# Moving pads, a mask and a sign guard between ScalarE, VectorE and GpSimd in a top-32 attention pipeline, with a new order of its steps

## The chip, the cores and the metric

The kernel runs on one core of a Trainium2 chip, as one launch. The metric is the device time of that launch in microseconds. TensorE is called PE here, its weight loads PEld, VectorE DVE, ScalarE ACT, GpSimd POOL and SyncE, which issues the transfers, SP, as the profile does. L305 is line 305 of the kernel before.

## What is computed

Three stages follow each other: attention that keeps the 32 largest scores of each row, a soft mixture of experts, and a two-layer network with a piecewise quadratic activation.

```python
B, H, S, D = 4, 8, 576, 64                     # attention
scores = (q @ k.T) / 8
kth = 32nd largest of each row
scores = where(scores >= kth, scores, -1e9)
x = softmax(scores) @ v                        # to (2304, 512)

logits = x @ phi                               # 8 experts x 4 slots
d = softmax(logits, axis=0); slots = d.T @ x
slots = relu(slots @ w1[e]) @ w2[e]            # 512 -> 1024 -> 512
x = softmax(logits, axis=1) @ slots

h = x @ w_in                                   # 512 -> 2048
g = where(h >= 1, h, where(h <= -1, 0, (h + 1)**2 / 4))
out = g @ w_out                                # 2048 -> 512
```

The weights `w_in` and `w_out` reach the chip as 64-bit numbers, so a step of the kernel turns them into 32-bit ones.

## The kernel before

**Tiling.** A unit of attention is a pair of heads, 16 in all (`NPAIR`), and a row group of 128 queries: groups 0 to 3 hold 128 queries of each of the two heads (j = 0, 1), group 4 the last 64 of both. The work on a group is cut into steps, each with a letter, a group and mostly a head: S11 is the scores of group 1 (there the second digit is a half of the columns), P30 the penalty of group 3, head 0.

**The steps of a group.** S: scores on PE (`op_s`). C: copy to SBUF on ACT (`op_c`, L296). G: the eight largest of each of seven segments on DVE (L305). L: from these, the 24 largest, on DVE (L312, L310). [...] X: scores once more on PE, with the masked ones pushed far down (`op_x`). Y: the next eight on DVE (L418), of which the last is the 32nd largest. Groups 3 and 4 (`BY_V`) take another way to Y: POOL multiplies scores and mask (V, L406). K: eight extra columns, the pad, from the count, so that ties and short counts come out right (`op_k`): on ACT for the V path and POOL's masks (L428), else on DVE (L430).

**The second half.** N: the largest score times -0.125, on POOL (L353), for the exponential. B: the 32nd largest times 2^100, on POOL (L441). P: a penalty for all that is smaller, on ACT (L445). U: its subtraction, on POOL (L448). E: exponential on ACT (L451). T, Q, R: transposes on PE and their copies on ACT. A: product with v on PE. H: copy of the result on ACT (L513). lD and lN, once per pair: the sum of each row plus 1e-9 and its reciprocal, on DVE (L532, L533), then the division on POOL (L536). The steps "m" are the softmax over the tokens of a batch, after its fourth pair; the last batch is treated apart.

**The conversion.** c0 to c6, once per pair, turn a 128 x 512 piece of `w_in` to 32 bits (`narrow`): Abs, low word and Sign on ACT (L225, L227, L229), a guard of the size and the reassembly on POOL (L231, L235, L237), a shift on DVE (L233). Its input is loaded by SP (L203), and its result stored (L217).

**What sets the order.** PE, ACT, DVE and POOL carry out their instructions in the order in which the steps are called, and that is the list `ORDER`, written out in the code. One pass through the list is a frame; the letter behind a step says how many frames it lags. So a frame mixes steps of up to five pairs:

```python
for frame in range(first, NPAIR + last + 1):
    for name, k in order:
        if frame == first == k and name[0] == "c":
            held.append(name)
        elif 0 <= frame - k < NPAIR:
            emit(name, frame - k)
            if name == "C20":
                while held:
                    emit(held.pop(0), 0)
    for name in held:
        emit(name, 0)
```

In the first frame the conversion's steps are held until C20 has been called or the frame ends. After the frames come the last batch's softmax (`moe_last`), the experts, the mixing and the network. Their weights are loaded by SP in one list (`wload`), each as soon as a buffer is given back; most buffers come free at the end of attention.

Of the kernel before, what the change touches and what calls it, by code (L numbers as in the profile page):

```python
# [64 lines left out]
Q40d B1c U01c M30c S40c E00c T41d C40c X20c G40c M31c P10c R4d S00b K21c P11c X21c me U10c Q41d  # L65
C00b Y20c E01c V30c T00c K30c Q00c S01b c4b C01b G00b c2b E10c Y21c U11c A40d T01c R0c B2c c5b
L4c V31c A41d S10b Q01c C10b Y30c P20c H4d X00b K31c E11c U20c S11b C11b T10c G01b A00c Q10c lDd
lNd c6b P21c A01c N3c E20c T11c Y31c H0c R1c M40c Q11c B3c U21c S20b V40c L0b K40c G10b C20b
M00b lYd lXd lEd P30c T20c S21b lCd z4b E21c A10c Q20c C21b A11c G11b T21c M01b K00b P31c H1c
N4c U30c Y40c L1b N1b O01b S30b G20b md R2c B4c me K01b X01b Q21c E30c A20c T30c md me M10b U31c  # L70
c0a C30b md me Y00b G21b A21c S31b Y01b E31c X10b L2b Q30c M11b P40c O11b H2c K10b c3a K11b me
T31c C31b B0b N0b U40c md M20b M21b P00b
# [6 lines left out]
def kernel_body(tc, qT, kT, vP, phi, w1, w2, w_in, w_out, out, fast, flag):  # L79
# [128 lines left out]
    def conv_op(i, k):  # L208
# [4 lines left out]
        if k == 2 and i + 1 < NCV:  # L213
            conv_load(i + 1)
# [4 lines left out]
    def narrow(x64, tr, sg, ops):  # L219
# [138 lines left out]
    def op_m(u, j):  # L358
# [4 lines left out]
        t = st[u]["t0"] + j  # L363
# [68 lines left out]
    def kth(u):  # L432
        return st[u]["l8"][:, :, PADS - 1] if fast else st[u]["top"][:, :, TOPK - 1]

    def op_b(u):
        n, t = width[u[1]], st[u]["t0"]
        if u[1] in BY_V:
            st[u]["kb"] = kth_all[:, t:t + n]
        else:
            st[u]["kb"] = p_small.tile([P, 2], F32, name="kb", tag="kb")  # L440
        nc.gpsimd.tensor_scalar(st[u]["kb"][:, :n], kth(u)[:, :n], BIG, None, op0=ALU.mult)  # L441

    def op_p(u, j):
# [6 lines left out]
    def op_e(u, j):  # L450
        nc.scalar.activation(row(u, j), row(u, j), AF.Exp, bias=st[u]["nm"][:, j:j + 1], scale=0.125)  # L451
# [282 lines left out]
    calls = dict(S=op_s, C=op_c, G=op_g, L=op_l, N=op_n, M=op_m, O=op_o, X=op_x, Y=op_y, K=op_k, B=op_b, P=op_p, U=op_u,  # L734
# [93 lines left out]
    if fast:  # L828
        cmp = p_moe.tile([P, NTILE], F32, name="cmp")
# [451 lines left out]
```

## Time and profile before

| | |
|---|---|
| timed runs | 803.58, 805.63, 807.99 us (median 805.63) |
| the profiled execution | 807.38 us, span 805.5 us, mean granted clock 0.983 of full |
| busy, share of the span | PE 94%, PEld 68%, DVE 81%, ACT 80%, POOL 57% |
| until 490 us (attention) | PE, DVE, ACT and POOL mostly at 0.9 or more, in tenths of a slice |
| 524 to 585 us | the 16 DMA engines full, 402 GB/s |
| from 585 us | PE 213 of 220 us |

The shares of the whole span are a mean over these stretches. A window gives the busy time of each engine in one stretch, overlaps counted once; what is left of the stretch is idle time, and the list of waits says which instruction of which engine ended most of it. Short gaps between small instructions are not listed there. Mean durations of a group of instructions overlap with those of their neighbours on the same engine by up to a tenth of a microsecond. PE's ends are modelled, so its busy time is an upper limit.

### The profile page before, as it was taken

The page shows a single profiled execution, that of the slowest core. Times are in us where ns is not written, and L with a number is a line of the kernel's source. Part 1 is how long each engine was busy: PE and PEld are TensorE (multiplying, and loading weights), DVE is VectorE, ACT ScalarE, POOL GpSimd, SP SyncE. Part 2 cuts the span into 40 slices and gives each one's busy share as a digit, 9 for nine tenths or more (in the row PEclk, how much of TensorE's full clock was granted, in tenths as well). Part 3 has the DMA queues.
Part 4 walks back from the last instruction along what each step waited for, and adds up shares of the span by engine and source line. Part 5 has one row for each costly group of instructions (what it writes and reads, how often), then busy time and mean ns, then how long its engine had stood idle before and what let it go on. Part 6 is the DMA issues. An engine that isn't in the chain of part 4 may idle for free.

```text
span 805.5 us, 15892 instructions
## 1 busy us (share of the span) xinstructions
PE 758.6 (94%) x5006; PEld 549.9 (68%) x5022; DVE 649.2 (81%) x2937; ACT 644.2 (80%) x1392; POOL 456.9 (57%) x482
## 2 busy tenths in 40 slices
PE   3799999999999999999999998898899999999996
PEld 1367677686777677767677777432477788888885
DVE  3999999999999999999999995153478876666662
ACT  3699999999999999999999997244399974545542
POOL 2699999998999999899999894002022200000000
PEclk9799999999999999999999999699999999999999
DMA  7234124224213222202202126599910020101001
GB/s 233 73 106 145 59 87 143 68 82 143 85 60 144 80 70 92 79 14 92 78 18 92 43 87 192 163 386 405 409 71 1 0 81 1 39 1 40 33 8 43
DMA packets 31726, 81.51 MB, mean 101 GB/s; under 512 B 5648, under 2 KB 6544, under 8 KB 31632
## 3 DMA queue, kind: packets, MB, share of 16 engines
q1 hardware_dynamic: 31344, 79.94, 28.2%
q8 instruction: 41, 0.67, 0.3%
q14 instruction: 53, 0.43, 0.2%
q10 hardware_dynamic: 288, 0.46, 0.2%
HBM read 71.25 MB, written 8.91 MB: 100 GB/s over the span
## 4 chain that ended last, share of the span: by engine, by line
PE 57%; DVE 18%; ACT 16%; POOL 4%; DMA 3%; issue 2%; SPq 1%; ACTq 0%; POOLq 0%; DVEq 0%
PE o_ps L1091 24%; PE av_ps L500 6%; PE s_ps L281 5%; PE pt_ps L459 5%; DVE cand L305 4%; ACT pen L445 4%; DVE l L418 4%; PE x_ps L281 3%; ACT ssb L296 3%; DVE cand L310 3%; DVE top L312 2%; PE h_ps L1055 2%; PE h L924 2%; POOL ssb L448 2%; DVE den L532 2%; DMA w<-in_moe_w_dram 2%
## 5 line engine op out<-in xcount | busy, mean ns | idle before, releaser
L1091 PE MATMUL o_ps<-whl,ghl 128*128 128x512 f32 x864 | 215.9, 394 | 0.0
L448 POOL TENSOR_TENSOR ssb<-ssb,pen 128x576 f32<-128x576 f32 x141 | 182.9, 1297 | 13.8 <-ACT pen L445 9.6
L1091 PEld LDWEIGHTS o_ps<-whl,ghl 128*128 128x128 f32 x864 | 160.7, 188 | 34.5 <-DVE ghl L1075 0.3
L305 DVE MAX8 cand<-ssb 128x8 f32<-128x82 f32 (+1 forms) x1008 | 165.1, 228 | 1.9 <-ACT ssb L296 1.9
L500 PE MATMUL av_ps<-v_sb,ptb 128*128 128x65 f32 (+1 forms) x1280 | 144.1, 262 | 0.0
L500 PEld LDWEIGHTS av_ps<-v_sb,ptb 128*128 128x128 f32 (+1 forms) x1280 | 138.8, 182 | 0.3
L281 PE MATMUL s_ps<-kt,qt 64*128 64x288 f32 x512 | 98.5, 462 | 15.5 <-ACT ssb L296 11.2
L451 ACT ACTIVATE ssb<-ssb,nm 128x576 f32<-128x576 f32 x141 | 111.8, 793 | 1.3 <-POOL ssb L448 0.9
L1057 ACT ACTIVATE rg<-h_ps,half 128x384 f32<-128x384 f32 x96 | 55.7, 580 | 67.8 <-PE h_ps L1055 67.8
L459 PE MATMUL pt_ps<-ident,ssb 128*128 128x128 f32 x640 | 100.9, 280 | 2.3 <-ACT ptb L475 0.9
L296 ACT COPY ssb<-s_ps 128x576 f32<-128x576 f32 x144 | 94.3, 655 | 7.4 <-PE s_ps L281 6.2
L1042 POOL TENSOR_TENSOR tr_l<-tr_l 128x512 int32<-128x512 int32 x16 | 20.9, 1307 | 130.1 <-PE so L947 46.2
L1063 DVE SCALAR_TENSOR_TENSOR rg<-h_ps,rg 128x384 f32<-128x384 f32 x96 | 53.3, 556 | 48.3 <-ACT rg L1058 48.3
L459 PEld LDWEIGHTS pt_ps<-ident,ssb 128*128 128x128 f32 x640 | 71.9, 146 | 29.8 <-ACT ptb L478 7.1
L369 POOL TENSOR_SCALAR mb<-ssb,top 128x576 bf16<-128x576 f32 x48 | 83.2, 1733 | 3.6 <-DVE top L312 3.6
L475 ACT COPY ptb<-pt_ps 128x512 f32<-128x512 f32 x128 | 77.6, 606 | 1.2 <-PE pt_ps L459 1.2
L418 DVE MAX8 l<-x_ps 128x8 f32<-128x584 f32 x96 | 73.0, 762 | 6.0 <-PE x_ps L400 6.0
L445 ACT ACTIVATE pen<-ssb,kb 128x576 bf16<-128x576 f32 x96 | 75.6, 788 | 2.1 <-POOL kb L441 1.8
L281 PEld LDWEIGHTS s_ps<-kt,qt 64*128 64x128 f32 x512 | 41.2, 191 | 51.2 <-ACT ssb L296 27.7
L312 DVE MAX8 top<-cand 128x8 f32<-128x56 f32 x432 | 73.2, 206 | 0.1
L406 POOL TENSOR_TENSOR w<-ssb,mb 128x576 f32<-128x576 f32 x48 | 61.5, 1282 | 0.1
L1075 DVE TENSOR_TENSOR ghl<-rg,ghl 128x384 fp32r<-128x384 f32 x96 | 55.2, 575 | 6.3 <-PE h_ps L1055 0.5
(220 smaller groups left out, 1306.8 us busy)
## 6 DMA issues: line engine op xcount, KB each, us to landing
w<-in_moe_w_dram SPq DMA_DIRECT2D x52, 512.0 KB, 6.4
x<-in_moe_w_in_dram SPq DMA_DIRECT2D x16, 512.0 KB, 4.9
w<-in_moe_w_out_dram SPq DMA_DIRECT2D x16, 512.0 KB, 10.2
w<-in_moe_w_dram SPq DMA_DIRECT2D x24, 256.0 KB, 4.7
kt<-in_k_dram SPq DMA_DIRECT2D x15, 360.0 KB, 3.0
v_sb<-in_v_dram SPq DMA_DIRECT2D x16, 325.0 KB, 4.8
qt<-in_q_dram SPq DMA_DIRECT2D x15, 320.0 KB, 3.5
out_dram<-o_sb SPq DMA_DIRECT2D x17, 256.0 KB, 2.5
```

The costliest lines, as they stand in the source:

```text
L281: nc.tensor.matmul(o, q[us], k[us, c:c + o.shape[-1]], start=True, stop=True, tile_position=(j * D, 0), skip_group_check=True)
L296: nc.scalar.copy(ssb[:, 0] if u[1] == NR else ssb[:, :, hf], st.pop((u, hf))[:, :, :HS])
L305: nc.vector.max(st[u]["cand"][:, j, 8 * g:8 * g + 8], row(u, j)[:, S * g // NSEG:S * (g + 1) // NSEG])
L312: nc.vector.max(t8, cand)
L369: nc.gpsimd.tensor_scalar(kept(u, j), row(u, j), t_u, None, op0=ALU.is_ge)
L418: nc.vector.max(st[u]["l8"][:, j], src)
L445: nc.scalar.activation(pen, row(u, j), AF.Relu, bias=st[u]["kb"][:, j:j + 1], scale=-BIG)
L448: nc.gpsimd.tensor_tensor(row(u, j), row(u, j), st.pop((u, "pen", j)), op=ALU.subtract)
L451: nc.scalar.activation(row(u, j), row(u, j), AF.Exp, bias=st[u]["nm"][:, j:j + 1], scale=0.125)
L459: nc.tensor.transpose(pt[:, c, :], pr[:, c0:c0 + P], ident)
L500: nc.tensor.matmul(o, pj[:, c, sl], v_sb[:, 4 * jj + c, :], start=False, stop=(c == NR - 1), skip_group_check=True)
L1091: nc.tensor.matmul(pos[t][n], a[:, sl], w, start=(f == 0 and k == 0), stop=(f == NF - 1 and k == 2))
```

## The change

Pads that ACT made are made on POOL (K for POOL's masks and for the V path), as a product with the count and a sum, in one instruction. The scaled maximum N goes; B multiplies the largest and the 32nd largest by -0.125 and 2^100 in one product with a table `factor`, into a tile `kn`. For that, Y writes its eight beside the 24 in `top`. One more mask, group 2, head 0, is made on POOL, so ACT counts it (O20). In the conversion, Abs and the guard on POOL go; DVE adds and subtracts 768 so that values under the guard become 0, ACT takes the sign of that, and the shift reads its input directly. The sum for den gets an accumulator that nothing reads. The counts are kept in smaller tables. The list is new.

```diff
-MASK_POOL = ((0, 1), (1, 1), (2, 1))
+MASK_POOL = ((0, 1), (1, 1), (2, 0), (2, 1))
+TINY = 1.5 * 2.0 ** 9
+NTOP = 6
 ORDER = '''
-X11c R3d me G30c Q31d E40d Y10c A30d G31c U00c c1b A31d P01c O21c Y11c L3c K20c H3d me N2c T40d
+A20c T30c C30b U31c O11b U40c Q30c Y01b A21c E31c L2b H2c S31b X10b B0b K10b C31b T31c c0a md
...
+    factor = p_moe.tile([P, 2, 2], F32, name="factor")
+    nc.vector.memset(factor[:, :, 0], -0.125)
+    nc.vector.memset(factor[:, :, 1], BIG)
...
-        if k == 2 and i + 1 < NCV:
+        if k == 4 and i + 1 < NCV:
             conv_load(i + 1)
...
             if k == 0:
-                nc.scalar.activation(tf, hf, AF.Abs)
+                nc.vector.tensor_scalar(sg, hf, TINY, TINY, op0=ALU.add, op1=ALU.subtract)
...
             elif k == 2:
-                nc.scalar.activation(sg, hf, AF.Sign)
-            elif k == 3:
-                nc.gpsimd.tensor_scalar(tf, tf, 2.0 ** -15, None, op0=ALU.max)
+                nc.scalar.activation(sg, sg, AF.Sign)
             elif k == 4:
-                nc.vector.tensor_scalar(t, t, 3, None, op0=ALU.logical_shift_left)
+                nc.vector.tensor_scalar(t, x64[:, :, 1], 3, None, op0=ALU.logical_shift_left)
...
-    def op_n(u):
-        n = width[u[1]]
-        nm = st[u]["nm"] = p_small.tile([P, 2], F32, name="nm", tag="nm")
-        nc.gpsimd.tensor_scalar(nm[:, :n], st[u]["top"][:, :n, 0], -0.125, None, op0=ALU.mult)
...
-        nc.vector.max(st[u]["l8"][:, j], src)
+        nc.vector.max(st[u]["top"][:, j, TOPU:], src)
...
         if v or (u[1], j) in MASK_POOL:
-            nc.scalar.activation(pad, ranks[:, 1 + v], AF.Identity, bias=ends_of[:, v:v + 1], scale=n)
+            nc.gpsimd.tensor_scalar(pad, ranks[:, 1 + v], n, (1.0, BIG)[v], op0=ALU.mult, op1=ALU.add)
         else:
-            nc.vector.tensor_scalar(pad, ranks[:, 0], n, 0.0, op0=ALU.subtract, op1=ALU.add, accum_out=ends_of[:, 2:3])
+            nc.vector.tensor_scalar(pad, ranks[:, 0], n, 0.0, op0=ALU.subtract, op1=ALU.add, accum_out=unread)
...
-        nc.gpsimd.tensor_scalar(st[u]["kb"][:, :n], kth(u)[:, :n], BIG, None, op0=ALU.mult)
+        nc.gpsimd.tensor_tensor(st[u]["kn"][:, :n], st[u]["top"][:, :n, 0:TOPK:TOPK - 1], factor[:, :n], op=ALU.mult)
...
-            nc.vector.tensor_scalar_add(den, xu_of[pi][:, :, D], 1e-9)
+            nc.vector.tensor_scalar(den, xu_of[pi][:, :, D], 1e-9, 0.0, op0=ALU.add, op1=ALU.add, accum_out=unread)
...
             if k == "P":
+                if j == 0:
+                    nm = st[u]["nm"] = p_small.tile([P, 2], F32, name="nm", tag="nm", bufs=2)
+                    n = width[r]
+                    nc.gpsimd.tensor_scalar(nm[:, :n], st[u]["top"][:, :n, 0], -0.125, None, op0=ALU.mult)
```

The new list has 168 entries for 173. Three places of it matter here. The first is ACT at the start of the program. Before:

```order
L578 COPY same<-pick_78 128x32 x4
L225 ACTIVATE tr<-x_191 128x512
L227 ACTIVATE tr<-x_191,two 128x512
L296 COPY ssb<-s_ps 128x2x288 x2
L229 ACTIVATE sg<-x_191 128x512
L296 COPY ssb<-s_ps 128x2x288 x4
```

After (L303 is the copy of scores, L232 the low word, L234 the Sign):

```order
L574 COPY same<-pick_78 128x32 x4
L303 COPY ssb<-s_ps 128x2x288 x5
L232 ACTIVATE tr<-x_192,two 128x512
L234 ACTIVATE sg<-sg 128x512
L381 ACTIVATE ones,cnt_all<-mb 128x576
```

The Abs and the low word of the first conversion stood ahead of the first copy of scores; the Abs is gone, and the low word and the Sign now stand behind the fifth copy. On DVE, at the same place, the rounding (L230) and the shift (L236) of the first conversion now follow the scans of the first group (L312), ahead of its selection (L319):

```order
L312 MAX cand<-ssb 128x8 x14
L230 TENSOR_SCALAR sg<-x_192 128x512
L236 TENSOR_SCALAR tr<-x_192 128x512
L319 MAX top<-cand 128x8 x2
L317 MATCH_REPLACE cand<-top,cand 128x56 x2
```

Before, the only one of the two, the shift, stood ahead of all scans. The third place is POOL in the middle of a frame, in the new order (L371 is a mask, L427 a pad, L444 the subtraction U, L437 the product B):

```order
L371 TENSOR_SCALAR mb<-ssb,top 128x576
L444 TENSOR_TENSOR ssb<-ssb,pen 128x576 x2
L437 TENSOR_TENSOR kn<-top,factor 128x4
L427 TENSOR_SCALAR mb<-ranks,cnt_all 128x8
L371 TENSOR_SCALAR mb<-ssb,top 128x576
L444 TENSOR_TENSOR ssb<-ssb,pen 128x576
L371 TENSOR_SCALAR mb<-ssb,top 128x576
L427 TENSOR_SCALAR mb<-ranks,cnt_all 128x8
L444 TENSOR_TENSOR ssb<-ssb,pen 128x576
L437 TENSOR_TENSOR kn<-top,factor 128x4
L427 TENSOR_SCALAR mb<-ranks,cnt_all 128x8
```

Between a mask and the pad that needs its count stand two or three instructions; before, POOL had no pads and went from a mask to other work.

## Rows read from the trace of the kernel before

**Rows 1.** Windows: us, then busy us (and instructions) of PE, PEld, DVE, ACT, POOL, PEclk, DMA share, GB/s.

```profile
102.03:131.39 29.36, 28.58 (x209) 20.77 (x211) 28.60 (x156) 29.16 (x65) 27.53 (x30) 1.00 0.29 99
160.75:191.24 30.49, 30.32 (x255) 22.96 (x257) 30.20 (x160) 30.40 (x71) 27.73 (x30) 1.00 0.34 111
524.00:585.00 61.00, 54.74 (x345) 21.75 (x337) 27.90 (x59) 24.79 (x49) 5.33 (x4) 1.00 1.02 402
```

**Rows 2.** Two lines of code: ns min/median/max, first and last start in us.

```profile
L532 DVE TENSOR_SCALAR den<-xu x15: 292/1249/1253, 72.7 to 485.3; 128x9 f32<-128x9 f32 x15
L233 DVE TENSOR_SCALAR tr<-tr x16: 407/412/1252, 14.2 to 453.7; 128x512 int32<-128x512 int32 x16
```

**Rows 3.** Groups, ACT and DVE, 102.03 to 458.53: xcount | busy us, mean ns | idle before.

```profile
L225 ACT ACTIVATE tr<-x 128x512 f32<-128x512 f32 x12 | 8.2, 680 | 0.1
L428 ACT ACTIVATE w<-ranks,ends_of,less_all 128x8 f32<-128x8 f32 x37 | 15.4, 416 | 0.0
L428 ACT ACTIVATE mb<-ranks,ends_of,cnt_all 128x8 bf16<-128x8 f32 x36 | 14.7, 408 | 0.0
L379 ACT ACTIVATE ones<-mb 128x576 bf16<-128x576 bf16 x36 | 24.6, 683 | 0.7
L379 ACT ACTIVATION_READ_ACCUMULATOR ones<-mb 128x1 f32 x36 | 7.1, 197 | 0.0
L371 DVE TENSOR_SCALAR_CACHE_REDUCE mb<-ssb,top 128x576 bf16<-128x576 f32 x36 | 28.8, 799 | 0.0
L430 DVE TENSOR_SCALAR_CACHE_REDUCE mb<-ranks,cnt_all 128x8 bf16<-128x8 f32 x36 | 7.3, 203 | 0.0
L430 DVE DVE_READ_ACCUMULATOR mb<-ranks,cnt_all 128x1 f32 x36 | 3.0, 83 | 0.0
L532 DVE TENSOR_SCALAR den<-xu 128x9 f32<-128x9 f32 x13 | 15.4, 1181 | 2.6 <-ACT xu L513 2.6
```

**Rows 4.** Timeline of POOL and DVE: start us, us, instruction, idle before it.

```profile
245.41 1.47 POOL L448 TENSOR_TENSOR ssb<-ssb,pen 128x576 f32<-128x576 f32 x1
...
250.05 1.29 POOL L448 TENSOR_TENSOR ssb<-ssb,pen 128x576 f32<-128x576 f32 x1 [0.27 <-ACT pen L445]
...
250.11 1.25 DVE L532 TENSOR_SCALAR den<-xu 128x9 f32<-128x9 f32 x1 [0.26 <-ACT xu L513]
```

**Rows 5.** Groups of POOL, 102.03 to 458.53.

```profile
L369 POOL TENSOR_SCALAR mb<-ssb,top 128x576 bf16<-128x576 f32 x36 | 62.4, 1734 | 0.0
L231 POOL TENSOR_SCALAR tr<-tr 128x512 f32<-128x512 f32 x12 | 17.9, 1493 | 0.0
...
L353 POOL TENSOR_SCALAR nm<-top 128x2 f32<-128x2 f32 (+1 forms) x60 | 13.4, 223 | 0.9
L441 POOL TENSOR_SCALAR kb<-l 128x2 f32<-128x2 f32 x36 | 8.0, 223 | 6.8 <-DVE l L418 4.4
```

**Rows 6.** Waits of POOL, same stretch: us in total, times, longest us.

```profile
POOL ssb L448 <- ACT pen L445: 8.2, 22, 0.9
POOL xh L536 <- DVE den L533: 5.1, 12, 0.4
POOL kb L441 <- DVE l L418: 4.4, 6, 1.1
```

**Rows 7.** Timeline of the program's start.

```profile
4.33 1.33 PE L281 MATMUL s_ps<-kt,qt 64*128 64x288 f32 x4 [4.33 <-DMA qt<-in_q_dram]
...
11.88 0.66 ACT L225 ACTIVATE tr<-x 128x512 f32<-128x512 f32 x1 [8.12 <-DMA x<-in_moe_w_in_dram]
...
13.07 0.64 ACT L296 COPY ssb<-s_ps 128x576 f32<-128x576 f32 x1
...
17.43 0.34 DVE L312 MAX8 top<-cand 128x8 f32<-128x56 f32 x2
...
19.12 1.75 POOL L369 TENSOR_SCALAR mb<-ssb,top 128x576 bf16<-128x576 f32 x1 [1.49 <-DVE top L312]
...
21.37 0.64 ACT L296 COPY ssb<-s_ps 128x576 f32<-128x576 f32 x1 [0.86 <-PE s_ps L281]
```

**Rows 8.** Timeline of DVE at the end of attention.

```profile
490.44 0.60 DVE L832 TENSOR_SCALAR less_all<-less_all 128x144 f32<-128x144 f32 x1 [1.56 <-ACT w L428]
```

More of the change, by code (lines that the diff above doesn't have):

```diff
@@ L59 @@
 NXH = 5
-MASK_POOL = ((0, 1), (1, 1), (2, 1))
+MASK_POOL = ((0, 1), (1, 1), (2, 0), (2, 1))
 NTR = 1
 NV = 2
+NTOP = 6
 ORDER = '''
-X11c R3d me G30c Q31d E40d Y10c A30d G31c U00c c1b A31d P01c O21c Y11c L3c K20c H3d me N2c T40d
[L65 to L72, printed above, removed]
+A20c T30c C30b U31c O11b U40c Q30c Y01b A21c E31c L2b H2c S31b X10b B0b K10b C31b T31c c0a md
+K11b z4b G30b M20b P00b X11b E40c Q31c U00b md G31b R3c S40b P01b c1a O20b T40c Y10b L3b Q40c
+A30c C40b M21b A31c E00b Y11b M30b K20b T41c O21b U01b G40b B1b H3c R4c K21b S00a V30b Q41c C00a
+X20b K30b X21b M31b P10b P11b c4a Y20b E01b U10b T00b Y30b Q00b S01a C01a G00a Y21b A40c E10b
+c2a A41c T01b H4c V31b L4b K31b Y31b Q01b B2b S10a X00a md R0b P20b G01a U11b me c5a lDc C10a
+U20b T10b md A00b Q10b E11b S11a P21b me lNc C11a E20b A01b T11b S20a H0b R1b lYc Q11b C20a L0a
+lXc M40b B3b T20b lEc M00a U21b V40b S21a P30b lCc Q20b G10a md M01a E21b K40b G11a O01a A10b
+A11b md K00a U30b K01a L1a Y40b mc C21a H1b P31b M10a T21b X01a G20a mc Y00a R2b c6a S30a Q21b
+B4b M11a E30b P40b mc G21a
 '''.split()
@@ L181, in kernel_body @@
         nc.vector.memset(ranks[:, 2, k:k + 1], -BIG / (S - TOPU - 0.5 - k))
-    ends_of = p_moe.tile([P, 3], F32, name="ends_of")
-    nc.vector.memset(ends_of[:, 0:1], 1.0)
-    nc.vector.memset(ends_of[:, 1:2], BIG)
-    phi_sb = p_moe.tile([P, NHP, 4, NSLOT], F32, name="phi_sb")
-    cnt_all = p_moe.tile([P, NTILE], F32, name="cnt_all")
-    less_all = p_moe.tile([P, NTILE], F32, name="less_all")
-    kth_all = p_moe.tile([P, NTILE], F32, name="kth_all")
+    unread = p_moe.tile([P, 1], F32, name="unread")
+    factor = p_moe.tile([P, 2, 2], F32, name="factor")
+    nc.vector.memset(factor[:, :, 0], -0.125)
+    nc.vector.memset(factor[:, :, 1], BIG)
+    width = [2] * NR + [1]
+    phi_sb = p_moe.tile([P, NHP, 4, NSLOT], F32, name="phi_sb")
+    n_v = sum(width[r] for r in BY_V)
+    n_x = sum(width) - n_v
+    cnt_all = p_moe.tile([P, NPAIR * n_x], F32, name="cnt_all")
+    less_all = p_moe.tile([P, NPAIR * n_v], F32, name="less_all")
+    kn_all = p_moe.tile([P, NPAIR * n_v, 2], F32, name="kn_all")
     if fast:
@@ L191, in kernel_body @@
         nc.vector.memset(less_all, S)
-        nc.vector.memset(kth_all, 1.0)
+        nc.vector.memset(kn_all, 1.0)
     raw = {}
@@ L268, in kernel_body, with at @@
     xu_of = {}
+    def at(u, j):
+        of_v = u[1] in BY_V
+        before = sum(width[r] for r in range(u[1]) if (r in BY_V) == of_v)
+        return u[0] * (n_v if of_v else n_x) + before + j
     def row(u, j):
@@ L376, in op_o @@
             return
-        t = st[u]["t0"] + j
+        t = at(u, j)
         ones = p_work.tile([P, S], BF16, name="ones", tag="ones", bufs=1)
@@ L450, in op_e @@
     def op_e(u, j):
-        nc.scalar.activation(row(u, j), row(u, j), AF.Exp, bias=st[u]["nm"][:, j:j + 1], scale=0.125)
+        nc.scalar.activation(row(u, j), row(u, j), AF.Exp, bias=st[u]["kn"][:, j, 0:1], scale=0.125)
     def op_t(u, j):
@@ L780, in last_pair @@
             else:
-                nc.vector.scalar_tensor_tensor(row(u, j), row(u, j), kth(u)[:, j:j + 1], st.pop((u, "pen", j)),
+                nc.vector.scalar_tensor_tensor(row(u, j), row(u, j), st[u]["top"][:, j, TOPK - 1:], st.pop((u, "pen", j)),
                                                op0=ALU.is_ge, op1=ALU.mult)
@@ L828, in kernel_body @@
     if fast:
-        cmp = p_moe.tile([P, NTILE], F32, name="cmp")
-        nc.vector.tensor_scalar(cmp, cnt_all, TOPK - 0.5, None, op0=ALU.is_gt)
-        bad = cpool.tile([P, 1], F32, name="bad")
-        nc.vector.tensor_scalar(less_all, less_all, S - TOPK + 0.5, None, op0=ALU.is_lt)
-        nc.vector.tensor_scalar(kth_all, kth_all, 0.0, None, op0=ALU.is_le)
-        nc.vector.tensor_tensor(cmp, cmp, less_all, op=ALU.max)
-        nc.vector.tensor_tensor(cmp, cmp, kth_all, op=ALU.max)
-        nc.vector.reduce_max(bad, cmp, axis=AX.X)
+        nc.vector.tensor_scalar(cnt_all, cnt_all, TOPK - 0.5, None, op0=ALU.is_gt)
+        nc.vector.tensor_scalar(less_all, less_all, S - TOPK + 0.5, None, op0=ALU.is_lt)
+        low = p_moe.tile([P, NPAIR * n_v], F32, name="low")
+        nc.vector.tensor_scalar(low, kn_all[:, :, 1], 0.0, None, op0=ALU.is_le)
+        nc.vector.tensor_tensor(low, low, less_all, op=ALU.max)
+        bad2 = p_moe.tile([P, 2], F32, name="bad2")
+        nc.vector.reduce_max(bad2[:, 0:1], low, axis=AX.X)
+        nc.vector.reduce_max(bad2[:, 1:2], cnt_all, axis=AX.X)
+        bad = cpool.tile([P, 1], F32, name="bad")
+        nc.vector.reduce_max(bad, bad2, axis=AX.X)
     att.close()
```

25 lines of the change are left out of this document (9 added, 16 removed).

## Prediction, before the changed kernel was run

> **What bounds the kernel now.** The profiled execution took 807.38 us for a span of 805.5; the three timed runs have a median of 805.63, so 1.75 is taken off whatever is summed against the profile. A measurement of this kernel can tell about 0.5%, or 4.0 us, from no change: 801.6 to 809.7 reads as "same".
>
> I read the busy tenths first: until about 490 us PE, DVE, ACT and POOL are all nearly full, from 520 to 585 DMA is, and after that PE. Nearly all that the change touches lies in the first stretch. The weights of the later stages start to load when buffers of attention come free, and 61 us of that run at 402 GB/s [rows 1]; I move everything behind attention as a block.
>
> Attention is a pipeline: one pass through the order list, a frame, per head pair. The addition for den stands once in a frame, 15 times from 72.7 to 485.3 [rows 2], so a frame takes 412.6/14 = 29.47 us. Windows cut at it show two kinds. A plain frame takes 29.36; in it ACT is busy for 29.16, DVE for 28.60, PE for 28.58 (its ends are modelled, an upper limit) and POOL for 27.53 [rows 1]. One that holds the expert softmax of a batch takes 30.49, with ACT at 30.40, DVE at 30.20 and POOL at 27.73 [rows 1]. ACT sets the pace, DVE is half a microsecond behind, POOL has 1.83 of room. Taking work off ACT alone is worth little more than the distance to the next engine, and part of it goes to POOL.
>
> **ACT per frame.** Out go the Abs of the conversion (0.680 us) and six pad instructions, three of 0.408 and three of 0.416 [rows 3]: 0.680 + 2.472 = 3.15. In comes the count of the fourth GpSimd mask, 0.683 + 0.197 [rows 3] = 0.88. The Sign stays, with another input. ACT falls from 29.16 to 26.9, or to 27.6 if the pads overlap their neighbours by a third. It no longer bounds.
>
> **DVE per frame.** Out go the fourth mask (0.799) and its pad (0.203) [rows 3]. The addition for den takes 1.181 on average for nine columns; the form with an accumulator I put at the pad's time and accumulator read, 0.203 + 0.083 [rows 3], so 0.90 goes. In comes the rounding of 512 columns, between 0.41, the undisturbed shift of 512 columns [rows 2], and 0.80, the mask of 576. I take 0.41, the nearer operation. 28.60 - 1.90 + 0.41 = 27.1.
>
> **DVE and POOL hold each other up.** That den's addition is slow has a reason in the rows: at 250.11 it lasts 1.25 and ends 0.02 after the POOL subtraction that began at 250.05 [rows 4]; its shortest, 0.292, and the shift's spread from 0.407 to 1.252 [rows 2] are of the same making. Masks with an accumulator show 0.799 in every stretch, so den should escape in that form. The shift stays as it is, and the new rounding is a second of its kind. Each can wait up to 0.84 (1.25 - 0.41); with both waits DVE is at 28.8 at most, about POOL's level below. My sum has no charge for it; the charge is a rival.
>
> **POOL per frame** is the term that decides. In comes the fourth mask at 1.734 and seven pad products (four for GpSimd masks, three for rows of the V path). No row has a pad on POOL; the nearest are the products of one or two columns at 0.223 and the mask, (1.734 - 0.223)/574 = 0.0026 per column [rows 5], so eight columns take some 0.24; bounds 0.22 and 0.31, the latter with the gap that small ones have behind them at times. I take 0.235, seven of them 1.645. Out go five scaled maxima at 0.223, 1.115, and the guard at 1.493 [rows 5]. The five threshold products stay, with twice the columns. 27.53 + 1.734 + 1.645 - 1.115 - 1.493 = 28.30.
>
> Of POOL's 1.83 of idle time, (8.2 + 5.1 + 4.4)/12 = 1.48 are listed waits [rows 6] and 0.35 are starts of small instructions, which remain: the floor is 28.65. The 0.43 for den goes with den's own wait. The other 1.05, for penalties from ACT and maxima from DVE, shrink when those engines have over a microsecond of room; I keep 0.4. A plain frame then takes 29.05, 0.3 less than now; bounds 28.65 (no wait left) and 30.1 (all 1.48 left). The heavy frame gains more, since its extra work is on ACT and DVE: ACT 28.1, DVE 28.7, POOL 27.73 + 0.77 + 0.35 = 28.85. I take 29.5, 1.0 less; bounds 0 and 1.6. Three of the 14 frames are heavy (the fourth batch is handled apart): 11 x 0.3 + 3 x 1.0 = **6.3 us**.
>
> **The start.** PE begins the first scores at 4.33 and takes 1.33, yet ACT copies them only at 13.07: the first conversion stands ahead of that copy in ACT's queue and its input lands at 11.88 [rows 7]. In the new order the copies come first, so ACT can begin at 5.7, 7.4 earlier. The wait does not vanish. Rounding and shift now stand on DVE between the first two candidate scans and the selection: the scans end near 10.1 instead of 17.43 [rows 7], DVE waits until 11.9, spends 0.8, and selects from 12.7: 4.7 earlier. POOL's first instruction is now the conversion's addition, behind five copies and a conversion on ACT. The fifth copy moves from 21.37 [rows 7] to 14.0; with 0.6, 0.8 and 1.3 for copy, conversion and addition, POOL's first mask starts near 16.7 instead of 19.12 [rows 7]: 2.4 earlier. DVE has selections and scans of the next row groups in between, so I take DVE's figure: **4.7 us**, bounds 2.4 and 7.4.
>
> **At nothing.** The tail's checks are seven small DVE instructions instead of six; the slowest now stands behind 1.56 of idle time [rows 8], and costs its 0.60 if that cover is gone. The scaled maximum of the last pair's two last row groups moves to just before its use: 0.22 each, bounds 0 and 0.6 together. Loads: SP issues the same transfers; the next conversion's input is asked for after this one's shift, a frame ahead of its use, and a pair's kt and qt 0.3 frames ahead, some 8 us, while the first input had landed 6 us after its issue among all the start's loads.
>
> **Sum.** 6.3 + 4.7 = 11.0; 807.4 - 11.0 = 796.4 for a run like the profiled one, less 1.75: **794.6 us**.
>
> **The rivals.**
> - *GpSimd reaches its floor*, 28.65 and 28.9: 11 x 0.7 + 3 x 1.6 + 4.7 = 17.2 less, **788.4**. For it: the other engines gain room, and ACT today idles only 0.2 in a plain frame. Against: each subtraction on POOL waits for an ACT penalty whose threshold POOL made. Chance 0.15.
> - *The two engines' mutual wait takes it back.* POOL is busy nearly always, so both unaccumulated DVE instructions meet it and then keep it out: the subtraction that met a shift took 1.47 instead of 1.29 [rows 4], and the whole 0.41 is possible. At 0.3 for each, less the 0.15 that POOL pays today, a plain frame takes 29.5 and a heavy one 29.9: 4.7 + 1.8 - 1.5 = 5.0 less, **800.6**, on the edge. Against: half of the shifts took at most 0.412 [rows 2], in the seam between two POOL instructions. Chance 0.20. The Trainium skill, page "SBUF — State Buffer", section "Who interferes with whom", says that a tensor_scalar between SBUF tensors which does not write out its accumulator can take ports that it shares with GpSimd, and that whichever of the two comes second is blocked until the other ends. The rows agree (0.292 against 1.25, 0.407 against 1.252); by that page den's escape is sure and the new rounding is a new blocker, the 800.6 of this rival rather than 794.6.
> - *The start gains little*: POOL's late first mask is the same wait in another place, 2.4, and the frames gain half, 3.2: 5.6 less, **800.0**. Chance 0.12.
> - *The pads stall GpSimd: slower.* Each of four pad products stands in POOL's queue and needs the count that ACT reads from a mask which POOL has just made; while it waits, subtractions and masks stand behind it. Two or three POOL instructions, 1.5 to 3 us, lie between mask and pad, for a count of 0.88 that stands in ACT's own queue. If each pad waits as long as a subtraction does now, 8.2/22 = 0.37 [rows 6], a plain frame takes 29.05 + 1.5 = 30.5 and a heavy one as much more: 14 x 1.5 = 21 on the forecast's frames, 10 slower, **815.6**. It decides from 11.0/(14 x 4) = 0.2 us per pad, where the whole gain is used up. Chance 0.10.
>
> The forecast has 0.43. Faster by over 0.5%: 0.43 + 0.15 + half of the mutual wait (0.10) + half of the small start (0.06) = 0.74; within 0.5%: the other halves, 0.16; slower 0.10. The range holds all but the stall and the outer ends of the bounds: 787 to 804.
>
> **What would show it.** Right: ACT's first copy near 5.7; den near 0.3 throughout; plain frames near 29.05 with POOL over 28.2 and ACT under 27.7; POOL's waits for den gone. Wrong: pads on POOL that wait for ACT's count; rounding or shift at 0.8 or more in most frames, with POOL subtractions of 1.45 behind them; or plain frames over 29.4 with POOL idle for more than 1 us in each.

## The result, and the profile after

The changed kernel has a median of 786.62 us (784.00 to 789.06), the kernel before 805.16 in the same series. The ratio is 0.9751, with an interval of 0.9721 to 0.9781: 2.5% faster, and 8 us below the forecast of 794.6, just under the range's lower end of 787. The profiled execution took 787.33 us with a span of 785.5, 20.0 less than before.

Two letters of the order list recur below. M is a mask of what belongs to the 24 largest. The masks on DVE count in the same instruction (TENSOR_SCALAR_CACHE_REDUCE in [rows 3]). The masks on POOL (`MASK_POOL`) are plain TENSOR_SCALARs in both kernels ([rows 5] and below), and ACT counts each of them in a step O; no run here makes a count on POOL.

The page of the profile, part 1 (busy us, share of the span, instructions), and then the windows of the same form as [rows 1]: a plain frame, a heavy one, the stretch in which DMA is full, and the rest.

```profile
PE 751.9 (96%) x5022; PEld 548.2 (70%) x5022; DVE 635.4 (81%) x2905; ACT 620.0 (79%) x1312; POOL 467.9 (60%) x516
```

```profile
94.60:123.20 28.60, 27.99 (x212) 20.59 (x210) 28.02 (x155) 27.74 (x60) 28.11 (x32) 1.00 0.32 109
151.80:181.20 29.40, 29.40 (x254) 22.32 (x253) 28.35 (x158) 28.61 (x65) 28.67 (x32) 1.00 0.30 102
504.00:566.00 62.00, 55.61 (x345) 22.96 (x336) 27.08 (x59) 24.88 (x49) 5.66 (x4) 0.97 1.02 401
566.00:785.50 219.50, 213.05 (x934) 173.33 (x933) 148.35 (x299) 139.81 (x263) 15.55 (x12) 0.99 0.07 24
```

The plain frame went from 29.36 to 28.60, the heavy one from 30.49 to 29.40 (the other two heavy ones are 29.03 and 29.04). ACT, which filled its frame to within 0.2 us, now has 0.86 idle; POOL, which had 1.83, has 0.49 and is the fullest engine whose ends are measured. The windows of the later stages show only that they nearly kept their lengths: from the last den to the end of the span it is 319.8 us, 320.2 before.

The line of the addition for den dates the frames, as in [rows 2]; beside it the new rounding (L230) and the shift (L236): ns min/median/max, first and last start.

```profile
L528 DVE TENSOR_SCALAR_CACHE_REDUCE den<-xu x15: 147/150/157, 66.0 to 465.7; 128x9 f32<-128x9 f32 x15
```

```profile
L230 DVE TENSOR_SCALAR sg<-x x16: 427/692/939, 11.6 to 424.3; 128x512 bf16<-128x512 f32 x16
L236 DVE TENSOR_SCALAR tr<-x x16: 420/1086/1102, 12.0 to 432.3; 128x512 int32<-128x512 int32 x16
```

The first den starts at 66.0 for 72.7, the 14 frames take 399.7 us for 412.6, and the end is 0.4 shorter: 6.7 + 12.9 + 0.4 = the 20.0 of the span. The minimum, median and maximum of a line are worth reading together: den is now 0.15 each time, while the shift, whose median was its minimum in [rows 2], now mostly takes 1.09.

POOL's groups from 94.6 to 438.8 us, twelve frames (columns as in [rows 5]):

```profile
L444 POOL TENSOR_TENSOR ssb<-ssb,pen 128x576 f32<-128x576 f32 x108 | 138.2, 1284 | 1.9
L371 POOL TENSOR_SCALAR mb<-ssb,top 128x576 bf16<-128x576 f32 x48 | 82.7, 1723 | 0.0
...
L427 POOL TENSOR_SCALAR mb<-ranks,cnt_all 128x8 bf16<-128x8 f32 x48 | 14.1, 294 | 0.0
...
L427 POOL TENSOR_SCALAR w<-ranks,less_all 128x8 f32<-128x8 f32 x36 | 10.8, 299 | 3.0
```

And all listed waits in that stretch, of POOL, DVE and ACT (us in total, times, longest). Waits under 0.15 us are not listed:

```profile
POOL w L408 <- DVE mb L368: 0.2, 1, 0.2
```

```profile
DVE top L418 <- POOL w L427: 4.7, 11, 0.6
DVE top L418 <- PE x_ps L402: 1.6, 5, 0.5
```

```profile
ACT ones L381 <- POOL mb L371: 4.3, 12, 0.5
ACT ptb L471 <- PE pt_ps L455: 1.9, 2, 1.1
ACT rs L479 <- PE rem_ps L461: 0.6, 3, 0.2
```

The direction has turned. In [rows 6] POOL waited for ACT and DVE; now ACT and DVE wait mostly for POOL, and POOL has one listed wait, of 0.2 us, in twelve frames. An engine that waits for nobody while its neighbours wait for it is the likely bound; the pads added and taken away below test it.

The start of the program, in the form of [rows 7]:

```profile
4.18 1.33 PE L288 MATMUL s_ps<-kt,qt 64*128 64x288 f32 x4 [4.18 <-DMA qt<-in_q_dram]
...
5.56 0.64 ACT L303 COPY ssb<-s_ps 128x576 f32<-128x576 f32 x1 [1.80 <-PE s_ps L288]
...
11.61 0.43 DVE L230 TENSOR_SCALAR sg<-x 128x512 bf16<-128x512 f32 x1 [1.61 <-DMA x<-in_moe_w_in_dram]
...
12.29 0.33 DVE L319 MAX8 top<-cand 128x8 f32<-128x56 f32 x2
...
17.05 1.75 POOL L371 TENSOR_SCALAR mb<-ssb,top 128x576 bf16<-128x576 f32 x1
```

The first copy comes 7.5 us earlier, the first selection 5.1 (17.43 before), POOL's first mask 2.1 (19.12 before): the wait for the conversion's input went from ACT to DVE, where it costs 1.61.

### The profile page after: what moved, and what is told of

Its sections match the earlier page's. It is cut to its first block, busy times and chain, and to the rows that moved or that the text cites. A ratio compares the mean times of both kernels' runs of the same rounds, so it can differ in the third digit from the quotient of the medians.

```text
span 785.5 us, 15901 instructions
## 1 busy us (share of the span) xinstructions
PE 751.9 (96%) x5022; PEld 548.2 (70%) x5022; DVE 635.4 (81%) x2905; ACT 620.0 (79%) x1312; POOL 467.9 (60%) x516
## 4 chain that ended last, share of the span: by engine, by line
PE 60%; DVE 23%; POOL 7%; ACT 6%; issue 2%; DMA 1%; ACTq 0%; POOLq 0%; DVEq 0%; SPq 0%
PE o_ps L1093 23%; PE av_ps L496 8%; DVE cand L312 7%; PE s_ps L288 6%; DVE top L418 5%; PE pt_ps L455 5%; POOL ssb L444 3%; PE x_ps L288 3%; DVE cand L317 2%; DVE top L319 2%; PE h L926 2%; PE h_ps L1057 2%; POOL mb L371 2%; DVE mb L368 2%; PE so L949 2%
## 5 line engine op out<-in xcount | busy, mean ns | idle before, releaser
L444 POOL TENSOR_TENSOR ssb<-ssb,pen 128x576 f32<-128x576 f32 x141 | 180.5, 1285 | 2.5
L312 DVE MAX8 cand<-ssb 128x8 f32<-128x82 f32 (+1 forms) x1008 | 163.8, 235 | 6.2 <-ACT ssb L303 6.2
L371 POOL TENSOR_SCALAR mb<-ssb,top 128x576 bf16<-128x576 f32 x64 | 110.3, 1723 | 0.9 <-DVE top L319 0.9
L288 PE MATMUL s_ps<-kt,qt 64*128 64x288 f32 x512 | 101.2, 473 | 8.6 <-ACT ssb L303 4.4
L303 ACT COPY ssb<-s_ps 128x576 f32<-128x576 f32 x144 | 95.6, 664 | 12.6 <-PE s_ps L288 10.4
L447 ACT ACTIVATE ssb<-ssb,kn 128x576 f32<-128x576 f32 x96 | 78.1, 813 | 0.7 <-POOL ssb L444 0.6
L441 ACT ACTIVATE pen<-ssb,kn 128x576 bf16<-128x576 f32 x96 | 75.1, 806 | 1.4 <-POOL kn L437 0.5
L418 DVE MAX8 top<-x_ps 128x8 f32<-128x584 f32 x96 | 72.7, 758 | 2.0 <-PE x_ps L402 1.6
L319 DVE MAX8 top<-cand 128x8 f32<-128x56 f32 x432 | 72.9, 205 | 0.1
```

The source lines that it names most:

```text
L288: nc.tensor.matmul(o, q[us], k[us, c:c + o.shape[-1]], start=True, stop=True, tile_position=(j * D, 0), skip_group_check=True)
L303: nc.scalar.copy(ssb[:, 0] if u[1] == NR else ssb[:, :, hf], st.pop((u, hf))[:, :, :HS])
L312: nc.vector.max(st[u]["cand"][:, j, 8 * g:8 * g + 8], row(u, j)[:, S * g // NSEG:S * (g + 1) // NSEG])
L319: nc.vector.max(t8, cand)
L371: nc.gpsimd.tensor_scalar(kept(u, j), row(u, j), t_u, None, op0=ALU.is_ge)
L418: nc.vector.max(st[u]["top"][:, j, TOPU:], src)
```

## The experiments

All ratios are against the kernel before, timed on the same chip. The changed kernel itself was timed only in the series of the result, so its 0.9751 (0.9721 to 0.9781) and the ratio of a variant are told apart only where their intervals are. "Plain" is the usual plain frame, from den to den.

### The start alone, and the start undone

**a_start_alone**: the kernel before, with the first pair's conversion held until the fifth copy has been called.

```diff
+        held, done = [], []
...
-            held = []
...
-                if frame == first == k and name[0] == "c":
+                if frame == k and name[0] == "c" and not done:
...
+                        done.append(frame)
...
-            for name in held:
-                emit(name, 0)
```

> The kernel before, with the first pair's conversion steps held until the fifth copy of scores; nothing else. Theory 'start': ACT copies the first scores near 5.6 us, the first den lands 5 to 7 us earlier than 72.7, frames stay at 29.36, and the whole is 5 to 7 us faster (ratio 0.991 to 0.994). Rival 'same wait elsewhere': DVE or GpSimd meet the late conversion, the first den gains 2.4 us or less (ratio 0.997 or more).

Measured: 802.72 us, ratio 0.9938 (0.9915 to 0.9962); first den at 69.7, 3.0 earlier, between what the two expectations named (the ratio is in the first one's range); the sum of the frames unchanged (412.6). Its timeline:

```profile
5.57 0.64 ACT L296 COPY ssb<-s_ps 128x576 f32<-128x576 f32 x1 [1.81 <-PE s_ps L281]
...
14.98 0.67 ACT L225 ACTIVATE tr<-x 128x512 f32<-128x512 f32 x1
...
17.27 0.43 DVE L233 TENSOR_SCALAR tr<-tr 128x512 int32<-128x512 int32 x1 [3.54 <-POOL tr L231]
```

The copy gains 7.5 us as in the changed kernel, but DVE's shift here still needs ACT's Abs and POOL's guard, and DVE waits 3.54 us for them. The wait moves along the chain; of the 7.5 us, 3.0 are left at the first den.

**b_start_undone**: the changed kernel, with the conversion not held.

```diff
-                if frame == first == k and name[0] == "c":
+                if False:
```

> The changed kernel, with the first pair's conversion no longer held, so that it stands ahead of the first copies again. Theory 'start': the first den moves from 66.0 back to about 72, frames stay at 28.5, and the whole loses 5 to 7 us against the changed kernel (ratio to the kernel before 0.982 to 0.985). Rival 'same wait elsewhere': it loses 2.4 us or less (ratio 0.978 or less).

Measured: 791.89 us, 0.9801 (0.9764 to 0.9837), between the two expectations. The first copy is at 12.80, the first den at 70.5, and the first 13 frames are those of the changed kernel to 0.03 us (the last is 0.18 shorter). So the held conversion is worth 70.5 - 66.0 = 4.5 us. The other 2.2 of the 6.7 are there without it; that the first frames, which are filled only in part, got shorter too is the likely reason, and k below points the same way: what makes its frames 2.65 longer also puts its first den 2.65 later, at 68.65.

### The list and the instructions, each without the other

**c_old_order**: the changed kernel's instructions in the list of before (N and c3 taken out, O20 put in).

```diff
-A20c T30c C30b U31c O11b U40c Q30c Y01b A21c E31c L2b H2c S31b X10b B0b K10b C31b T31c c0a md
+X11c R3d me G30c Q31d E40d Y10c A30d G31c U00c c1b A31d P01c O20c O21c Y11c
...
```

> The changed kernel's instructions in the old list (without its entries for the scaled maximum and the guard, and with the count of the fourth mask right ahead of the count of the third). Theory 'GpSimd floor': GpSimd's work per frame sets it whatever the list, plain frames come to 28.5 to 28.8 and only the start's 6 us are lost (ratio 0.980 to 0.986). Rival 'order': the old list leaves GpSimd waiting for penalties and maxima as before, 1 us or more of listed waits per frame, and plain frames stay at 29.2 or more (ratio 0.993 or more).

Measured: 818.46 us, 1.0121 (1.0082 to 1.0160): slower than before, plain frame 29.89. Waits of POOL from 110 to 440 us:

```profile
POOL mb L429 <- ACT ones L383: 13.7, 11, 1.9
POOL ssb L446 <- ACT pen L443: 5.1, 13, 1.0
```

This is the prediction's slower rival, though in the old list: a pad at the head of POOL's queue waits up to 1.9 us for ACT's count. Its total price was nearly right (10 us slower than before; here 1.2%), its form was not: about one pad of the four waits in each frame, 13.7/11 = 1.2 us, not each of them for 0.37. Of the two expectations the rival 'order' holds, but the longer waits are for counts, not for penalties and maxima as before.

**d_new_order_old_instr**: the instructions of before in the new list, with N and c3 put in where B and the low word stand.

```diff
+A20c T30c C30b U31c O11b U40c Q30c Y01b A21c E31c L2b H2c S31b X10b N0b B0b
...
-X11c R3d me G30c Q31d E40d Y10c A30d G31c U00c c1b A31d P01c O21c Y11c L3c K20c H3d me N2c T40d
...
```

> The kernel before with the new list: each scaled maximum ahead of its threshold product, the guard behind the low word, three GpSimd masks, pads on ACT as before. Theory 'both are needed': ACT's 29.16 us of work keep plain frames at 29.2 to 30; with the start's 4 to 5 us the ratio is 0.990 to 1.005. Rival 'the list alone': frames come to 28.5 to 28.8 with the old instructions too (ratio 0.975 to 0.980).

Measured: 819.62 us, 1.0146 (1.0121 to 1.0172), plain frame 30.1. Waits of POOL, same stretch:

```profile
POOL ssb L450 <- ACT pen L447: 18.9, 11, 2.1
POOL xh L538 <- DVE top L314: 2.9, 8, 0.4
```

With the pads and the guard's Abs still on ACT, one of the new list's subtractions in each frame comes some 1.7 us (18.9/11) before its penalty is ready. No engine is full there: in a plain frame of 30.1 ACT is busy for 29.17 and POOL for 27.49. That is slower than both expectations (ratio 1.005 at most). Neither half gains anything in the frames: the medians are 1.2% and 1.5% slower, both together 2.5% faster.

### What a pad costs GpSimd

**k_pads_twice**: the changed kernel, each of the seven pads made twice.

```diff
-            nc.gpsimd.tensor_scalar(pad, ranks[:, 1 + v], n, (1.0, BIG)[v], op0=ALU.mult, op1=ALU.add)
+            for _ in range(2):
+                nc.gpsimd.tensor_scalar(pad, ranks[:, 1 + v], n, (1.0, BIG)[v], op0=ALU.mult, op1=ALU.add)
```

> The changed kernel with each of the seven GpSimd pads of a frame made twice. Theory 'GpSimd floor': GpSimd has no idle time to hide them in, so seven times 0.23 to 0.27 us, 1.6 to 1.9, is added to each plain frame (30.1 to 30.4), 23 to 27 us in all. Rival 'port': VectorE's blocked instructions set the frame and GpSimd has room; 0.5 us or less per frame, 7 us or less in all.

Measured: 828.00 us, 1.0257 (1.0216 to 1.0298). The line of the pads, and a plain frame:

```profile
L428 POOL TENSOR_SCALAR mb<-ranks,cnt_all x128: 260/270/554, 19.1 to 498.8; 128x8 bf16<-128x8 f32 x128
L428 POOL TENSOR_SCALAR w<-ranks,less_all x96: 270/270/341, 32.7 to 511.4; 128x8 f32<-128x8 f32 x96
```

```profile
100.00:131.25 31.25, 28.66 (x211) 20.59 (x213) 28.04 (x156) 28.19 (x60) 30.11 (x39) 1.00 0.27 93
```

Seven instructions more: POOL is busy 2.00 us longer (0.29 each), but the frame is 2.65 longer (0.38 each) where 1.6 to 1.9 was expected, with no listed wait of POOL. The rest is in short gaps. It is the price of a second copy right behind the first: in the changed kernel itself the four pads for masks have no gap before them and the three of the V path 3.0/36 = 0.08 each. Heavy and plain frames are now alike (31.2 to 31.3): with POOL as far behind as this, the extra work of a heavy frame on the others disappears. That shows that what is added to POOL is paid in full and a little more.

**h_one_pad_act**, **h2_v_pads_act** and **n_pad_act_but_heavy** take the other direction: pads of the V path back to ACT, one (group 4's), three, or group 4's in three pairs of four.

```diff
-        if v or (u[1], j) in MASK_POOL:
+        if u[1] == NR:
+            nc.scalar.activation(pad, ranks[:, 1 + v], AF.Identity, bias=pend[:, v:v + 1], scale=n)
+        elif v or (u[1], j) in MASK_POOL:
```

(`pend` holds 1 and 2^100; the condition is `if v:` for three, and `if u[1] == NR and u[0] % NHP != 0:` for the last.)

> The changed kernel with one of the seven GpSimd pads of a frame, that of the fourth group's V row, back on ACT. GpSimd has 0.3 to 0.4 us less per frame, ACT 0.3 to 0.4 more (27.7 to 28.1). Theory 'GpSimd floor': plain frames fall by 0.2 to 0.4 to 28.2 to 28.4 and the whole by 3 to 5 us (ratio 0.969 to 0.972). Rival 'balanced already': VectorE at 28.0 and the list hold the frame, no change (ratio 0.975).

> The changed kernel with all three pads of the V path back on ACT. GpSimd has 1.0 us less per frame (27.1), ACT 0.9 to 1.2 more (28.6 to 28.9). Theory 'the next engine sets it': frames stay between 28.5 and 29.0 with ACT as the limit, ratio 0.974 to 0.985. Rival 'GpSimd alone': frames fall to 28.2 or less (ratio 0.968 or less).

> The changed kernel with the fourth group's V pad on ACT in three pairs of four, and on GpSimd in the pair whose pad falls into the frame with the expert softmax, where ACT was the limit when all of them stood on ACT. Theory 'each frame has its own limit': plain frames at 28.15 as with that pad on ACT, heavy ones at 29.0 to 29.4 as in the changed kernel, 5 to 6 us faster than the changed kernel (ratio 0.967 to 0.971). Rival 'the list evens it out': what a plain frame gains the heavy one waits for, ratio 0.973 or more.

Measured: one 786.51 us, 0.9737 (0.9718 to 0.9755); three 791.35, 0.9803 (0.9784 to 0.9822); one but for every fourth pair 785.73, 0.9732 (0.9711 to 0.9753). The plain and a heavy frame with one pad on ACT:

```profile
93.05:121.18 28.13, 27.87 (x211) 20.64 (x210) 27.98 (x155) 27.84 (x61) 27.81 (x31) 1.00 0.31 106
263.62:293.45 29.83, 29.78 (x254) 22.42 (x254) 28.80 (x158) 29.21 (x67) 28.23 (x31) 1.00 0.29 103
```

One pad less on POOL makes its busy time 0.30 and the plain frame 0.46 shorter; with k, that shows POOL as the bound of the plain frame. But the second and third heavy frames take 29.83 and 29.84 for 29.03 and 29.04, and the time stays. In the one shown POOL is busy for only 28.23, so POOL does not bound it. With three, plain frames are 28.06, under what was expected, and heavy ones 30.7. Sparing the pair that was thought to meet the softmax keeps the heavy frames at 29.03 to 29.39, as expected, but only four plain frames gain 0.45 to 0.48 and come to 28.15; each of the others changes by 0.31 less to 0.19 more. The sum of all frames is 397.5 us for 399.7, where eleven times 0.45 would be 5 less. The first den is 0.5 earlier, and the interval overlaps the changed kernel's. No version here is shown to beat it.

### Room on the neighbours

**l_low_word_twice**: the changed kernel, with the conversion's low word made twice on ACT.

```diff
-                nc.scalar.activation(r.bitcast(F32), x64[:, :, 0].bitcast(U32), AF.Identity, bias=two, scale=2.0 ** -51)
+                for _ in range(2):
+                    nc.scalar.activation(r.bitcast(F32), x64[:, :, 0].bitcast(U32), AF.Identity, bias=two, scale=2.0 ** -51)
```

> The changed kernel with the low word of the conversion made twice on ACT, 0.66 us more per frame (27.7 to 28.4). Theory 'room on the others ends GpSimd's waits': ACT still has 0.2 us of room, but GpSimd's waits for penalties and counts come back in part, plain frames 28.8 to 29.2. Rival 'the list has the slack': frames stay within 0.1 of 28.6.

Measured: 796.21 us, 0.9870 (0.9844 to 0.9895), plain frame 29.23 with ACT busy for 28.43 and POOL for 28.20. POOL's waits, 110 to 440 us:

```profile
POOL mb L428 <- ACT ones L382: 6.2, 16, 0.5
```

ACT had 0.86 us of room in a plain frame; 0.7 of work on it costs 0.63, and it still has 0.80 idle. Where the work stands explains it. In the changed kernel ACT goes without idle time from the low word through two counts (L381), and the pad that needs the second follows closely:

```profile
112.22 0.75 ACT L232 ACTIVATE tr<-x,two 128x512 f32<-128x512 uint32 x1
...
115.57 0.20 ACT L381 ACTIVATION_READ_ACCUMULATOR ones<-mb 128x1 f32 x1
...
116.03 0.29 POOL L427 TENSOR_SCALAR mb<-ranks,cnt_all 128x8 bf16<-128x8 f32 x1
```

The count ends 0.26 before its pad starts. A second low word, 0.7 more work ahead of it, is more than that, and the same pad then waits 0.46. Idle time elsewhere in ACT's frame does not cover it.

**g_three_masks**: the fourth mask, its pad and its count back on DVE. The step O20 also goes from the list.

```diff
-MASK_POOL = ((0, 1), (1, 1), (2, 0), (2, 1))
+MASK_POOL = ((0, 1), (1, 1), (2, 1))
```

> The changed kernel with the fourth mask, its pad and its count back on VectorE (three masks on GpSimd). GpSimd has 2.0 us less per frame, ACT 0.9 less, VectorE 0.9 to 1.0 more, 28.0 to 29.0. Theory 'two engines near the limit': VectorE then sets the frame, 28.9 to 29.4 (ratio 0.980 to 0.993). Rival 'GpSimd alone': frames fall to 28.2 or less (ratio 0.968 or less).

Measured: 794.71 us, 0.9838 (0.9802 to 0.9874); plain frame 28.84, heavy ones up to 30.3. A plain frame of it, and POOL's two longest waits from 110 to 440 us:

```profile
97.70:126.55 28.85, 28.26 (x211) 20.50 (x209) 28.82 (x159) 27.38 (x58) 26.39 (x30) 1.00 0.29 103
```

```profile
POOL kn L437 <- DVE top L418: 12.1, 14, 1.9
POOL ssb L444 <- ACT pen L441: 8.3, 12, 0.9
```

DVE is full (28.82 of 28.85) and POOL waits for its maxima. In the frames the fourth mask is worth 406.7 - 399.7 = 7.0 us, the largest of the parts that were undone one by one. Not undone by themselves were all seven pads together, the merged product B, and Abs and guard.

### Two changes on DVE

**e_no_rounding**: ACT takes the sign of the input itself; the rounding goes. The next input's load is also asked for earlier, after the Sign instead of after the shift.

```diff
-        if k == 4 and i + 1 < NCV:
+        if k == 2 and i + 1 < NCV:
...
-                nc.vector.tensor_scalar(sg, hf, TINY, TINY, op0=ALU.add, op1=ALU.subtract)
+                pass
...
-                nc.scalar.activation(sg, sg, AF.Sign)
+                nc.scalar.activation(sg, hf, AF.Sign)
```

> The changed kernel without the rounding on VectorE: the Sign reads the input again, so the guard of very small values is left out. Theory 'GpSimd floor': VectorE's blocked time was beside GpSimd's work; a plain frame loses at most what one blocked meeting costs GpSimd, 0 to 0.2 us (28.4 to 28.6, ratio 0.970 to 0.976). Rival 'port': the blocked rounding holds the frame, 0.4 us or more per frame goes (28.2 or less, ratio 0.968 or less).

Measured: 784.22 us, 0.9704 (0.9678 to 0.9729), an interval that overlaps the changed kernel's; the frames' sum is 397.7 us for 399.7, or 0.14 a frame, the plain one 28.37 for 28.60. A plain frame:

```profile
94.10:122.46 28.36, 27.98 (x211) 20.59 (x210) 27.43 (x155) 27.62 (x60) 27.88 (x32) 1.00 0.28 96
```

POOL is busy for 27.88 instead of 28.11: 0.23 less, as much as the frame.

**f_den_undone**: den in the form of before.

```diff
-            nc.vector.tensor_scalar(den, xu_of[pi][:, :, D], 1e-9, 0.0, op0=ALU.add, op1=ALU.add, accum_out=unread)
+            nc.vector.tensor_scalar_add(den, xu_of[pi][:, :, D], 1e-9)
```

> The changed kernel with den's addition in its old form, without the accumulator. Theory 'VectorE's room counts': VectorE is busy 28.0 of 28.6 us, so 0.9 to 1.1 us of waiting for GpSimd and a GpSimd wait behind it lengthen each frame by 0.4 us or more (29.0 or more, ratio 0.982 or more). Rival 'GpSimd alone': VectorE takes it in its idle time, frames stay within 0.1 us of 28.6 (ratio 0.975).

Measured: 787.35 us, 0.9743 (0.9706 to 0.9780), frames' sum 399.3 for 399.7. Its den line:

```profile
L528 DVE TENSOR_SCALAR den<-xu x15: 158/480/820, 66.1 to 465.4; 128x9 f32<-128x9 f32 x15
```

In the new list, den no longer falls beside a whole subtraction each time (median 0.48, was 1.25), and DVE has room for what is left. The accumulator, which makes it 0.15 + 0.08, is worth nothing that shows.

## Why the prediction was right or wrong

**Right: the mechanism.** ACT stopped being the bound, POOL became it in the plain frames, and ACT's first copy stands at 5.56 (forecast 5.7). "Copies, scans, selection from 12.7" was 12.29, POOL's first mask "near 16.7" 17.05. The slower rival (pads that wait for counts) is real, as c shows, and the new list is what keeps it out: in the changed kernel no pad's wait is listed in twelve frames. Of the signs named, ACT is at 27.74, just over the 27.7, and POOL at 28.11, just under the 28.2. ACT's six pads had been taken at their recorded 0.41; counted only from the end of the record before, they filled about 0.25 each.

**Wrong: "I keep 0.4".** The step that failed is what was left of POOL's waits. The prediction had 28.30 busy, 0.35 of starts and 0.4 of waits, 29.05. Measured are 28.11 busy and 0.49 idle, listed waits among it 0.2 us in twelve frames, that is 0.02 a frame: 28.60. So the waits are 0.38 lower than forecast, the busy time 0.19 lower, the starts 0.12 higher. Over 11 plain frames the gain was 8.9 us (12.9 less the heavy frames' 4.0) for a forecast of 3.3, the largest part of what was missed.

The 0.35 came from a mixed reading: it takes 1.48, an average over twelve frames of both kinds, from the 1.83 of one plain frame. That frame itself lists

```profile
POOL ssb L448 <- ACT pen L445: 0.9, 3, 0.4
POOL xh L536 <- DVE den L533: 0.4, 1, 0.4
```

so 1.3 were waits and 0.5 were starts and other short gaps, and 0.49 is what is left after the change.

The rival "GpSimd reaches its floor", with a chance of 0.15 and 788.4 us, is what happened in the plain frames. That its 28.65 is so near the 28.60 is in part luck: its busy time was too high and its starts too low. The argument against it was that each subtraction waits for a penalty whose threshold POOL made; in the changed kernel the penalty is there in time. Why is only shown in part. By c and d it takes both the moved work and the new list. Room on ACT and DVE by itself does not decide: h has no listed wait of POOL in its plain frame with ACT idle for 0.29 and DVE for 0.15, while in l ACT is idle for 0.80 and POOL waits for counts. In g, with DVE full, the waits for maxima and penalties of [rows 6] are back.

**Mis-sized: the heavy frames,** 1.1, 1.45 and 1.4 us less where 1.0 was taken (bound 1.6): 4.0 for 3.0. What limits them is not settled. PE's modelled busy time fills all three (29.40 of 29.40, 29.03 of 29.03 and 29.04 of 29.04, an upper limit), and h moved the first down by 0.4 and the others up by 0.8 with one 8-column product a frame. PE as their bound was not tested.

**Mis-sized: the start,** 6.7 us for 4.7, inside the bounds. The term itself was right: b gives 4.5. The 2.2 that b keeps lie before the first den, which the sum left out but for the start: it counted 14 frames from the first den on, though the pairs that fill the pipeline ahead of it pass through the new list too.

**Right by errors that cancel: POOL's busy time.** The pads were put at 0.235 and are recorded at 0.294 and 0.299; h and k give 0.29 to 0.30 of busy time each. Seven of them are 0.4 dearer than forecast, yet the frame's busy time is 0.19 below the sum. Records overlap, so I count each POOL record of the two plain frames only from the end of the one before. So counted, the pads take 1.88, 0.23 more than forecast, and the five maxima free 0.14 less. Against that the nine subtractions take 11.26 instead of 11.58, which the sum had held constant (0.18 of it is the one that took 1.47 beside the shift), and about 0.1 less each go to the fourth mask, to the products B, and to conversion and division together.

**The mutual wait came, and cost POOL little.** DVE paid: the rounding's median is 0.69 and the shift's 1.09, where 0.41 was taken for each; that is 0.28 + 0.68, and lifts the estimate of 27.1 to about the 28.02 measured. POOL, for which the rival charged 0.3 each, paid less, and not in its subtractions (a mean of 1.284, 1.267 to 1.434). The small instruction behind the blocked one paid. In the plain frame:

```profile
108.58 0.89 DVE L230 TENSOR_SCALAR sg<-x 128x512 bf16<-128x512 f32 x1
...
109.14 0.39 POOL L437 TENSOR_TENSOR kn<-top,factor 128x4 f32<-128x4 f32 x1
...
115.86 0.21 POOL L437 TENSOR_TENSOR kn<-top,factor 128x4 f32<-128x4 f32 x1
```

The rounding meets a subtraction and ends at 109.47; the product behind that subtraction takes 0.39, another one 0.21. The pad behind the shift takes 0.34 instead of 0.27. That is about 0.25 a frame, where POOL paid 0.18 before, and e gives 0.23 back in its plain frame (0.14 in the mean of all) without the rounding. The Trainium skill, page "SBUF — State Buffer", section "Who interferes with whom", says that of the two engines whichever comes second to the ports they share is blocked. The trace agrees for both sides (DVE: 0.42 against 1.09 for the same shift, and 0.15 each time for the form with an accumulator; POOL: 0.21 against 0.39 for the same product). The rival's plain frame was 29.5, and measured is 28.60: its price of 0.3 for each on POOL was too high, and the forecast's 29.05 under it was too high as well.

**Nothing: "0.90 goes" for den.** The estimate of the engine's time was good, but by f it is worth no time. It was part of why POOL's 0.43 of waits for den would vanish; they vanish in f as well (its POOL lists no wait for den).

**At nothing, and rightly:** tail, loads and the last pair's products, 0.4 us less in all; they were not told apart.

## What to carry to other kernels

When work moves from a full engine to one with room, forecast the new bound by its busy time plus its gaps, and read both from the same frame. For its old waits, look at what stands in its producers' queues right ahead of what it needs, and not at how long they are idle: 0.7 us more work on an engine with 0.86 idle cost 0.63, since it stood ahead of a count that the bound needed 0.26 us later. Where the engines take instructions in a list's order, moved work and list are one change: here each alone was slower (1.2% and 1.5%), both together 2.5% faster. And count the frames that fill the pipeline, too.

## What was not expected of the hardware

- A small GpSimd product of eight columns takes 0.26 to 0.30 us in the records, but a second one right behind the first, on a full GpSimd, cost 0.38 us of the frame (run k: 2.65/7), 0.09 of it in gaps that no listed wait explains.
- VectorE's 128 x 512 shift of 32-bit numbers takes 0.42 us or about 1.09 beside GpSimd, and the rounding of as many columns 0.43 to 0.94, while GpSimd's subtractions beside them stay within 1.43 (before, the longest was 1.51) and the four-column product behind a blocked rounding takes 0.39 instead of 0.21.
- The addition for den, nine columns, takes 0.15 us each time with an accumulator and 0.16 to 0.82 without, in the same list.
